# Attention and gated MLP on one core: a new order of the work, the bias loaded first, w_out later, and the last output tiles in two goes

## The chip, the cores and the metric

The kernel runs on one core of a Trainium2 chip. The core has five engines with queues of their own, each of which works its instructions off in order: TensorE (PE in the profile; its weight loads are PEld) for matmuls, VectorE (DVE), ScalarE (ACT), GpSimd (POOL) and SyncE (SP), which here only issues DMAs. The metric is the device time of one execution in microseconds (us), the median of several runs.

## The reference, cut to what matters

Four batches, eight heads, 768 positions, head size 64; the positions form eight blocks of 96.

```python
P = sort_net                                    # [4, 8, 8, 8]
for _ in range(5):                              # Sinkhorn
    P = np.exp(P - P.max(-1, keepdims=True))
    P = P / P.sum(-1, keepdims=True)
    P = P / P.sum(-2, keepdims=True)
k_sorted = einsum('bhij,bhjcd->bhicd', P, k_b)  # blocks of k and v mixed by P
v_sorted = einsum('bhij,bhjcd->bhicd', P, v_b)
scores = q_b @ k_sb.T / 8                       # inside each block of 96
x = softmax(scores) @ v_sb                      # then heads side by side: [4, 768, 512]

h = relu(x @ w_in)                              # [4, 768, 1024]
u, v = h[..., :512], h[..., 512:]
v_n = (v - mean(v)) / sqrt(var(v) + 1e-6)
v_s = einsum('ts,bsd->btd', w_spatial, v_n) + b_spatial[None, :, None]
out = (u * v_s) @ w_out                         # [4, 768, 512]
```

## The kernel before, in words

The work is cut into small units, functions named `u_XX`, and the string `ORDER` lists them one after another: `SC:2:1:0:1` calls `u_SC` with the PSUM bank 2, batch 1, head pair 0, half 1. The order is written out by hand; no scheduler moves anything. Each engine gets its instructions in the order in which the units issue them, and waits only where data or a buffer are not ready. So a unit that stands early in the list and whose data are late holds back everything behind it on its engine. A letter A, D or P in a unit names the engine that takes the result out of PSUM or works on it: ScalarE, VectorE or POOL. PSUM has eight banks, used mostly in pairs (0, 2, 4, 6).

The units of one batch:

- Loads (`L`, `LH`, lines 152 to 212) are issued by POOL and cast from fp32 to bf16 on the way. `LH` loads q by four heads.
- Head of the program only: `SK` is one Sinkhorn step (one exp on ScalarE, six operations on VectorE), `MK` makes a mask, `SX` a selector, `PR` (line 258) spreads P with eight small matmuls, `P0` (line 265) multiplies the mask by P into `pd[0]`, the mixing matrices of batch 0, on VectorE. `PC` copies the spread P to SBUF and `PD` makes the matrices of batches 1 to 3 on POOL. `DM` are dummy matmuls on a zero tile.
- `QT` (318) turns q of a head pair, `KT` (346) mixes and turns k, each with 12 matmuls and one copy. `VT` (357) does the same with v of batch 0 and `VX` (374) turns it back by halves into `vb`. For batches 1 to 3, `VM` (386) mixes v of a head pair in two matmuls and `VC` (400) moves it to `vb` by four DMAs of 99 KB on SP's queue, one for each block; `VC:b:0` and `VC:b:1` are the halves.
- For batches 2 and 3, `QX` (171) replaces `QT`: q is reordered by two copies (VectorE or POOL) and turned by one DMA transpose on SP's queue. `WT` (302) is a one-element copy on POOL that waits for that transpose, so that the loads behind it on POOL do not start before.
- `SC` (410) makes the scores of a head pair and half of the blocks (8 matmuls) and their exp on ScalarE, `AT` (439) multiplies them with `vb` (8 matmuls, line 448, one for each block and head) and divides by the sums (VectorE, or ScalarE, VectorE and POOL for P).
- x is turned by `XT` (TensorE, batch 0) or `XX` (DMA transpose on SP's queue, the others).
- `VP` (484) computes the v half of x @ w_in, one or two tiles of 128 positions, relu, statistics; `LN` the root, `LA` (515) normalizes a tile in place; `UP` (528) computes the u half; `WS` (293) turns w_spatial.
- `SP` (543) computes one quarter of w_spatial @ v_n in 12 matmuls, adds the bias (`z`, line 554) and multiplies by u (`gt`, 560): the gate. `SH` (563) does this for one half of the positions. `OP` (591) computes two tiles of the output from the four gates of a batch, copies and stores them; `OH` (579) one tile.

The batches overlap: attention of batch b+1 is interleaved with the MLP of batch b. SP's queue holds, in order, the load of P, the eight `VC` of batch 1, the bias, then for each batch two `XX`, the q transpose, the eight `VC`, and the output stores. The last units are `SP:6:D:3:2 SP:4:D:3:0 SP:6:P:3:1 SH:4:D:3:3:1 SH:5:D:3:3:0`, then six `OH`.

Of the kernel before, what the change touches and what calls it, by code (L numbers as in the profile page):

```python
# [8 lines left out]
FP32 = mybir.dt.float32  # L9
# [51 lines left out]
def kernel(  # L61
# [34 lines left out]
    moe = ctx.enter_context(tc.tile_pool(name="moe", bufs=2))  # L96
# [33 lines left out]
    mask16 = const.tile([128, TB], BF16, name="mask16")  # L130
# [100 lines left out]
    def u_MK():  # L231
        nc.vector.reduce_sum(out=m32, in_=ident.rearrange("p (j t) -> p t j", t=TB), axis=AX.X)
        nc.vector.tensor_copy(out=mask16, in_=m32)
        for n in range(NE):
            nc.vector.memset(ex[n][:, 2 * NI * BLK:], 0.0)

    def u_IV(n):
        n = int(n)
# [35 lines left out]

    def u_PC(eng):
# [287 lines left out]
    def u_SH(ps, gate, b, mc, x):  # L563
# [12 lines left out]
        eng = nc.vector if gate == "D" else nc.gpsimd  # L576
        eng.tensor_mul(out=st["gt", b, mc][:, cols], in0=z, in1=st["u", b, mc // 2][:, mc % 2, cols])

    def u_OH(ps, eng, b, c):
        b, c = int(b), int(c)  # L580
        t = ps_tile(ps)
        for mc in range(FC):
            nc.tensor.matmul(
                t[:, 0, :], lhsT=st["gt", b, mc][:, c * 128:(c + 1) * 128], rhs=w_out_sb[:, mc, :],
                start=(mc == 0), stop=(mc == FC - 1),
            )
# [58 lines left out]
```

## Time and profile before

| | us |
|---|---|
| median of 13 runs | 159.59 (158.27 to 162.24) |
| profiled execution | 159.21 |
| its span | 157.2 |
| TensorE busy | 141.8 |
| VectorE, ScalarE, POOL busy | 118.0, 83.5, 53.8 |
| first matmul, last matmul's end | 6.5, 152.7 |

The span runs from the first instruction to the last; the rest of the 159.21 us lies around it. Matmuls overlap in time, so a busy TensorE is not TensorE at its peak; chains of units are better read from the timeline. A DMA's row (`SPq`, or POOL for the loads) is the time in which it is issued; its landing comes later and is shown by whoever waits for it.

### The profile page before, as it was taken

The numbers are of one execution on the slowest core, as the hardware profiler recorded it, in microseconds if no ns is written. First come the engines' busy times: TensorE is split into PE (matmuls) and PEld (weight loads), VectorE is DVE, ScalarE is ACT, GpSimd is POOL, SyncE is SP. The second block draws the span as 40 slices with busy tenths as digits, with TensorE's granted clock in tenths as the row PEclk, the third lists the DMA queues.
The fourth block names the chain that finished last, engine by engine and source line by source line (L and its number), as shares of the span: only waits on it lengthen the run. The fifth ranks groups of instructions, "written<-read, shape, count | busy, mean of one in ns | idle before, by whom it ended". The sixth has DMA issues, their size and how long they took to land.

```text
span 157.2 us, 3919 instructions
## 1 busy us (share of the span) xinstructions
PE 141.8 (90%) x1617; PEld 88.3 (56%) x1617; DVE 118.0 (75%) x231; ACT 83.5 (53%) x127; POOL 53.8 (34%) x78
## 2 busy tenths in 40 slices
PE   0399989899998999999899979999999999999880
PEld 0397878546776665645556644655566545556330
DVE  3865889599896789489786999775688679649830
ACT  3234989588877526666654325787751234410130
POOL 7961930747400260240740660062201401500400
PEclk9999999999999999999999999999999999999998
DMA  1999999999999999989999989741554503052073
GB/s 14 194 204 204 207 210 209 203 204 206 243 271 213 205 164 140 201 115 210 216 295 253 154 146 184 123 88 55 216 157 77 100 4 133 0 188 79 0 262 141
DMA packets 36689, 25.49 MB, mean 162 GB/s; under 512 B 16576, under 2 KB 33472, under 8 KB 36672
## 3 DMA queue, kind: packets, MB, share of 16 engines
q0 software_dynamic: 14864, 12.19, 49.9%
q1 hardware_dynamic: 21808, 13.06, 36.1%
q8 instruction: 12, 0.20, 0.5%
q14 instruction: 5, 0.04, 0.1%
HBM read 24.78 MB, written 6.29 MB: 198 GB/s over the span
## 4 chain that ended last, share of the span: by engine, by line
PE 52%; DMA 24%; DVE 11%; POOL 4%; issue 4%; SPq 3%; ACT 1%; DVEq 0%; ACTq 0%; POOLq 0%
PE ps L548 14%; DMA wsp_nat<-in_moe_w_spatial_dram 13%; PE ps L491 10%; PE ps L536 10%; DMA vb<-vm 9%; PE ps L597 8%; DVE z L554 4%; PE ps L448 3%; SPq L405 3%; DVE gt L560 2%; PE ps L423 2%; PE ps L339 2%; DMA out_dram<-oh_sb 1%; DVE stats L505 1%; DVE v_sb L116 1%
## 5 line engine op out<-in xcount | busy, mean ns | idle before, releaser
L548 PE MATMUL ps<-wspT,v_sb 128*128 128x384 bf16 x180 | 31.2, 326 | 0.0
L436 ACT ACTIVATE ex<-ps 96x768 bf16<-96x768 f32 x32 | 24.5, 806 | 10.8 <-PE ps L423 10.8
L536 PE MATMUL ps<-xT,w_in_sb 128*128 128x384 bf16 x128 | 23.0, 326 | 0.8 <-DMA xT<-x_sb 0.5
L491 PE MATMUL ps<-w_in_sb,xT 128*128 128x512 bf16 x96 | 22.7, 379 | 0.5 <-DVE z L554 0.5
L548 PEld LDWEIGHTS <-v_sb 128*128 128x128 bf16 x180 | 17.0, 98 | 10.9
L460 POOL TENSOR_TENSOR x_sb<-xr,rec 96x512 bf16<-96x512 f32 x8 | 8.3, 1040 | 37.7 <-DVE rec L459 37.7
L554 DVE TENSOR_TENSOR z<-ps,b_bc 128x768 f32<-128x768 f32 x15 | 14.3, 953 | 5.4 <-PE ps L548 5.3
L505 DVE BATCH_NORM_STATS2 stats<-v_sb 128x6 f32<-128x512 bf16 x24 | 16.3, 678 | 2.6 <-ACT v_sb L114 2.1
L536 PEld LDWEIGHTS <-w_in_sb 128*128 128x128 bf16 x128 | 12.1, 98 | 9.0 <-issue 1.1
L460 DVE TENSOR_TENSOR x_sb<-ps,rec 96x512 bf16<-96x512 f32 x24 | 16.5, 687 | 0.8
L597 PE MATMUL ps<-w_out_sb,gt 128*128 128x512 bf16 x72 | 16.9, 379 | 0.0
L522 POOL TENSOR_SCALAR v_sb<-v_sb,nm,rstd 128x512 bf16<-128x512 bf16 x15 | 12.1, 806 | 8.5 <-issue 5.4
L491 PEld LDWEIGHTS <-xT 128*128 128x128 bf16 x96 | 9.0, 98 | 10.4 <-issue 0.7
L114 ACT ACTIVATE u_sb<-ps 128x768 bf16<-128x768 f32 x12 | 9.7, 811 | 9.3 <-PE ps L536 9.1
L560 DVE TENSOR_TENSOR gt<-z,u_sb 128x768 bf16<-128x768 f32 x12 | 13.6, 1137 | 0.4
L116 DVE TENSOR_SCALAR v_sb<-ps 128x1024 bf16<-128x1024 f32 (+1 forms) x9 | 9.9, 1100 | 4.5 <-PE ps L491 4.4
L108 ACT CAST vm<-ps 128x768 bf16<-128x768 f32 x11 | 8.5, 804 | 7.6 <-PE ps L390 7.5
L448 PE MATMUL ps<-vb,ex 96*128 96x65 bf16 x256 | 11.9, 193 | 0.7 <-DMA vb<-vm 0.7
L448 PEld LDWEIGHTS <-ex 96*128 96x128 bf16 x256 | 10.0, 97 | 3.5 <-issue 0.9
L521 POOL TENSOR_SCALAR nm<-mv 128x1 f32<-128x1 f32 x15 | 3.0, 199 | 24.7 <-DVE mv L506 18.5
L108 ACT CAST kT<-ps 128x768 bf16<-128x768 f32 x10 | 8.0, 804 | 5.5 <-PE ps L339 5.5
L108 ACT COPY o_sb<-ps 128x1024 f32<-128x1024 f32 x7 | 7.1, 1012 | 6.8 <-PE ps L597 6.6
(91 smaller groups left out, 205.8 us busy)
## 6 DMA issues: line engine op xcount, KB each, us to landing
out_dram<-o_sb SPq DMA_DIRECT2D x9, 512.0 KB, 3.0
k_in<-in_k_dram POOLq DMA_DIRECT2D x4, 768.0 KB, 19.9
v_in<-in_v_dram POOLq DMA_DIRECT2D x4, 768.0 KB, 15.4
vb<-vm SPq DMA_DIRECT2D x24, 99.0 KB, 4.7
q_in<-in_q_dram POOLq DMA_DIRECT2D x3, 768.0 KB, 20.1
out_dram<-oh_sb SPq DMA_DIRECT2D x6, 256.0 KB, 2.0
wsp_nat<-in_moe_w_spatial_dram POOLq DMA_DIRECT2D x1, 1152.0 KB, 20.4
w_in_sb<-in_moe_w_in_dram POOLq DMA_DIRECT2D x2, 512.0 KB, 14.4
```

What stands on the lines that cost most here:

```text
L108: nc.scalar.copy(out=out, in_=in_)
L436: nc.scalar.activation(out=dst, in_=src, func=AF.Exp, scale=scale)
L448: nc.tensor.matmul(t[:, hh, ii * VW:ii * VW + D + 1], lhsT=e[:, c:c + 128], rhs=vb[b % 2][:, ih * NI + ii, 2 * hp + hh, 0:D + 1], start=Tr ...
L460: (nc.gpsimd if eng == "P" else nc.vector).tensor_mul(out=x_sb[:, hp].rearrange("p i (h d) -> p h i d", h=2), in0=tv[:, :, :, 0:D], in1=_r ...
L491: nc.tensor.matmul(t[:, x, :], lhsT=x_tile(b, n // 3)[:, kc, n % 3 * 128:(n % 3 + 1) * 128], rhs=w_in_sb[:, kc, DH:DFF], start=(kc == 0), ...
L505: nc.vector.bn_stats(out=stats, in_=v_sb[:, x, :])
L522: nc.gpsimd.tensor_scalar(out=v_sb, in0=v_sb, scalar1=nm[:, 0:1], scalar2=rs[:, n:n + 1], op0=ALU.add, op1=ALU.mult)
L536: nc.tensor.matmul(t[:, x, 0:HW], lhsT=w_in_sb[:, kc, mc * 128:(mc + 1) * 128], rhs=x_tile(b, ih)[:, kc], start=(kc == 0), stop=(kc == KC ...
L548: nc.tensor.matmul(t[:, x, 0:HW], lhsT=st["v_sb", b, n][:, mc * 128:(mc + 1) * 128], rhs=wspT[:, n, x * HW:(x + 1) * HW], start=(n == 0), ...
L554: nc.vector.tensor_add(out=z.rearrange("p (x c) -> p x c", x=2), in0=t[:, :, 0:HW], in1=b_bc.rearrange("p (x c) -> p x c", x=2),)
L560: eng.tensor_mul(out=gt, in0=z, in1=st["u", b, mc // 2][:, mc % 2])
L597: nc.tensor.matmul(t[:, x, :], lhsT=st["gt", b, mc][:, c * 128:(c + 1) * 128], rhs=w_out_sb[:, mc, :], start=(mc == 0), stop=(mc == FC - 1),)
```

## The change

The string `ORDER` is new from end to end: the same units of attention and MLP in another sequence, with other banks and other engines for some. The parts that have names:

- The bias (`BB`) is issued on SP behind the load of P; it was issued behind the `VC` of batch 1.
- `w_out` (`L:wo`) is loaded behind q of the third batch (b=2) instead of between q of b=1 and v of b=2.
- `P0` takes two heads and all eight rows of P instead of four heads and four rows.
- `VT` mixes a whole head pair's v at once (`ih` = 2: N=128), four units instead of eight with N=64; `VX` stays by halves.
- In the tail, one half of the last gate (`SH:7:D:3:3:1`) stands ahead of the three `SP`, all three of these multiply on VectorE, and the output tiles are made in two goes: `OF` multiplies gates 0 and 1, `OL` adds gates 2 and 3, copies and stores. The last tile is copied by halves, on ScalarE and VectorE, and stored by two DMAs, from ScalarE's queue and SP's.
- q of the fourth batch is reordered by VectorE (`QX:D:3`) instead of POOL; `LA` on POOL goes from 15 to 11, `AT` with P from 8 to 10, `SP` with P from 3 to 5.
- The clearing of the tails of `ex` moves from `u_MK` to `u_IN`.

```diff
-IN SK:0 LH:q:0:0:4 L:k:0:0:128 ID MK SK:0 L:v:0:0:128 SK:0 QT:0:A:0:1:2 SK:0 QT:2:A:0:0:2 DM:0:12:64
-LH:q:0:4:8 DM:1:12:64 SX L:wv DM:0:12:64 DM:1:12:64 SK:1 DM:0:12:64 DM:1:12:64 PR:0 P0:1:4:8 IV:1
-P0:0:4:8 P0:1:0:4 P0:0:0:4 DM:7:5:384 KT:1:A:0:2:2 PC:A KT:3:A:0:3:2 VT:7:D:1:0 IV:0 VT:5:A:2:0
...
-SC:2:0:3:1 PD:1:4:8 SC:0:0:2:1 L:q:1:0:128 L:wo AT:6:D:0:3:0 VX:4:D:2:1 XT:2:A:0:1:0 XT:3:D:0:0:0
-XT:7:D:0:0:1 AT:0:P:0:3:1 L:v:2:0:128 AT:4:D:0:2:1 WS:2:A:1 WS:3:A:3 VP:6:D:0:0:1 XT:0:A:0:1:1
...
-SC:4:1:3:1 LA:P:0:4 BB AT:0:D:1:1:1 UP:2:A:0:1:0 AT:6:D:1:2:1 AT:4:P:1:3:1 SP:0:D:0:1 SC:4:1:2:0
-AT:6:P:1:3:0 SP:2:P:0:0 XX:1:1 AT:6:D:1:2:0 XX:1:0 QX:D:2 VM:4:A:2:0 SP:0:D:0:3 KT:6:A:2:1:2
-VM:4:A:2:3 SP:2:D:0:2 VM:4:A:2:1 VM:0:A:2:2 VP:6:A:1:4:5 UP:0:A:1:1:1 UP:4:A:1:0:0 KT:0:A:2:2:2
-LN:1:4:6 VC:2:0 KT:6:D:2:3:2 KT:2:D:2:0:2 VP:4:D:1:2:3 SC:2:2:2:0 SC:6:2:0:0 VC:2:1 VP:0:D:1:0:1
-WT:q:2:0 L:v:3:0:128 SC:6:2:3:1 SC:2:2:1:0 L:k:3:0:128 OP:4:A:0:2 AT:2:D:2:2:0 L:q:3:0:128 LN:1:0:4
-LA:P:1:1 AT:0:D:2:0:0 LA:P:1:0 LA:D:1:5 OP:6:A:0:1 LA:P:1:4 AT:4:P:2:3:1 UP:2:D:1:0:1 SC:6:2:3:0
...
-SP:6:D:3:2 SP:4:D:3:0 SP:6:P:3:1 SH:4:D:3:3:1 SH:5:D:3:3:0 OH:7:A:3:3 OH:5:D:3:4 OH:4:A:3:0
-OH:7:D:3:5 OH:5:A:3:1 OH:4:A:3:2
+IN LH:q:0:0:4 L:k:0:0:128 ID SK:0 MK L:v:0:0:128 SK:0 SK:0 IV:1 QT:0:A:0:1:2 DM:0:12:64 SK:0
+DM:1:12:64 DM:0:12:64 SK:1 SX DM:1:12:64 QT:2:A:0:0:2 DM:0:12:64 PR:1 P0:0:2 DM:7:9:64 KT:2:A:0:0:2
+LH:q:0:4:8 L:wv P0:2:4 P0:4:6 L:wu IV:0 DM:7:1:64 KT:4:A:0:2:2 P0:6:8 KT:6:D:0:1:2 DM:0:1:64
+VT:2:A:3:2 PC:A L:ws L:v:1:0:128 VT:4:D:0:2 KT:6:D:0:3:2 VX:0:D:3:0 VT:1:A:1:2 QT:4:A:0:3:2 PD:3:0:4
...
+VX:0:D:2:0 XT:1:D:0:1:0 SC:4:0:0:0 XT:2:D:0:1:1 AT:6:D:0:2:0 AT:0:D:0:3:0 AT:4:D:0:0:0 UP:2:A:0:1:1
+VP:7:A:0:5 XT:0:A:0:0:1 WS:2:A:3 XT:4:A:0:0:0 VP:6:D:0:3:4 VM:2:A:1:0 VM:0:A:1:3 VP:4:D:0:2
...
+QT:2:A:1:2:2 LA:P:0:4 QT:6:D:1:1:2 UP:4:D:0:0:0 SC:6:1:3:1 SC:2:1:1:1 WS:0:D:1 L:k:2:0:128 WS:1:D:2
+L:q:2:0:128 SC:4:1:2:1 VC:1:1 QT:6:D:1:0:2 KT:2:A:1:0:2 AT:0:D:1:3:1 LA:P:0:1 SC:4:1:3:0 VC:1:0
+AT:6:D:1:1:1 SC:2:1:0:1 WS:0:D:4 VM:4:A:2:1 AT:6:D:1:2:1 SC:2:1:0:0 LA:P:0:0 L:wo AT:0:D:1:0:1
+LA:P:0:2 SC:4:1:2:0 AT:6:D:1:3:0 LA:P:0:5 AT:2:P:1:0:0 SC:0:1:1:0 KT:4:A:2:1:2 XX:1:1 AT:2:D:1:2:0
+SP:6:P:0:0 AT:4:D:1:1:0 VM:2:A:2:3 XX:1:0 QX:D:2 SP:0:P:0:2 VM:4:A:2:0 VM:2:A:2:2 SP:6:D:0:3
+SP:2:D:0:1 UP:6:A:1:0:1 KT:2:D:2:2:2 KT:0:D:2:3:2 KT:4:A:2:0:2 VP:6:A:1:0:1 UP:0:A:1:1:1 SC:6:2:3:0
+SC:4:2:0:1 VP:2:D:1:4:5 SC:6:2:2:1 VC:2:0 VC:2:1 SC:0:2:3:1 OP:4:A:0:2 AT:0:D:2:3:0 AT:2:D:2:0:1
+LN:1:4:6 VP:6:D:1:2:3 WT:q:2:0 L:v:3:0:128 SC:0:2:1:1 SC:4:2:2:0 L:k:3:0:128 L:q:3:0:128 UP:2:A:1:0:0
...
+UP:2:D:3:0:0 LA:D:3:3 OP:0:A:2:2 LA:P:3:2 SH:7:D:3:3:1 SP:2:D:3:0 SP:0:D:3:1 SP:2:D:3:2 SH:0:D:3:3:0
+OF:7:3:0 OF:2:3:5 OF:3:3:4 OL:A:3:4 OL:D:3:5 OF:0:3:3 OL:A:3:0 OL:D:3:3 OF:2:3:2 OL:A:3:2 OF:7:3:1
+OL:X:3:1
...
     def u_IN():
         nc.sync.dma_start(out=p_all, in_=sort_net.rearrange("b h i j -> (b h) i j"))
...
+        for n in range(NE):
+            nc.vector.memset(ex[n][:, 2 * NI * BLK:], 0.0)
...
-    def u_P0(ih, lo, hi):
+    def u_P0(lo, hi):
...
         nc.vector.tensor_mul(
-            out=pd[0][:, lo:hi, ih * 64:ih * 64 + 64].rearrange("p h (i t) -> p h i t", t=TB),
-            in0=_raw_ap(mask16, 0, [mask16.ap[0], [0, n], [0, NI], [1, TB]]),
-            in1=_raw_ap(pr, lo, [pr.ap[0], [1, n], [BH, NI], [0, TB]]),
+            out=pd[0][:, lo:hi].rearrange("p h (i t) -> p h i t", t=TB),
+            in0=_raw_ap(mask16, 0, [mask16.ap[0], [0, n], [0, NB], [1, TB]]),
+            in1=_raw_ap(pr, lo, [pr.ap[0], [1, n], [BH, NB], [0, TB]]),
         )
...
+    EARLY, LATE = (0, 1), (2, 3)
+
+    def oh_mm(b, c, parts):
+        for mc in parts:
+            nc.tensor.matmul(
+                st["oh", c][:, 0, :], lhsT=st["gt", b, mc][:, c * 128:(c + 1) * 128], rhs=w_out_sb[:, mc, :],
+                start=(mc == EARLY[0]), stop=(mc == LATE[-1]),
+            )
+
+    def u_OF(ps, b, c):
+        st["oh", int(c)] = ps_tile(ps)
+        oh_mm(int(b), int(c), EARLY)
...
+    def u_OL(eng, b, c):
+        b, c = int(b), int(c)
+        oh_mm(b, c, LATE)
+        t = st["oh", c][:, 0]
+        o_sb = oh_tile()
+        dst = out[b, c * 128:(c + 1) * 128, :]
+        if eng in ("A", "D"):
+            copy(eng, o_sb, t)
+            nc.sync.dma_start(out=dst, in_=o_sb)
+        else:
+            h = DM // 2
+            o2 = moe.tile([128, S], FP32, name="o2", tag="z", bufs=2)[:, 0:h]
+            nc.scalar.copy(out=o_sb[:, 0:h], in_=t[:, 0:h])
+            nc.vector.tensor_copy(out=o2, in_=t[:, h:DM])
+            nc.scalar.dma_start(out=dst[:, 0:h], in_=o_sb[:, 0:h])
+            nc.sync.dma_start(out=dst[:, h:DM], in_=o2)
```

## The prediction

> **What bounds the kernel now.** I read the page first, then TensorE's busy time by stage, then its waits, then the queues around the one DMA wait that the change moves, last the end of the timeline.
>
> The page's busy times of the engines:
> ```profile
> PE 141.8 (90%) x1617; PEld 88.3 (56%) x1617; DVE 118.0 (75%) x231; ACT 83.5 (53%) x127; POOL 53.8 (34%) x78
> ```
> Busy time by stage (start:end, length, then the engines in the page's order, granted clock, DMA share, GB/s):
> ```profile
> 6.50:13.40 6.90, 6.65 (x111) 5.88 (x113) 4.72 (x22) 1.88 (x4) 3.96 (x9) 1.00 1.31 204
> 13.40:28.30 14.90, 13.44 (x353) 11.71 (x352) 12.41 (x29) 13.12 (x21) 5.91 (x6) 1.00 1.23 207
> 28.30:138.60 110.30, 108.22 (x1085) 63.93 (x1086) 86.99 (x150) 64.10 (x94) 36.93 (x51) 1.00 0.88 162
> 138.60:157.20 18.60, 13.44 (x73) 6.75 (x71) 10.41 (x12) 2.35 (x4) 1.64 (x1) 0.96 0.38 141
> ```
> From 28.3 to 138.6 us TensorE is busy for 108.2 of 110.3 us: what it loses there is lost for good, and work removed elsewhere is worth nothing. Before 28.3 ScalarE and VectorE are nearly full (13.1 and 12.4 of 14.9) beside full DMAs. The tail is a chain of its own. TensorE's own waits:
> ```profile
> PE ps L324 <- DMA q_in<-in_q_dram: 6.5, 1, 6.5
> PE ps L448 <- DMA vb<-vm: 0.7, 2, 0.4
> PE ps L583 <- POOL gt L560: 0.6, 1, 0.6
> PE ps L536 <- DMA xT<-x_sb: 0.5, 1, 0.5
> PE ps L491 <- DVE z L554: 0.5, 1, 0.5
> ```
> The second line is the one to watch. The third batch's V goes to `vb` by eight DMAs on SP's queue, behind the transpose of q. The timeline of SP and POOL, then TensorE's and the chain's rows:
> ```profile
> 59.25 4.71 SPq L183 DMA_TRANSPOSE qX<-qx  x1
> 64.05 5.99 SPq L405 DMA_DIRECT2D vb<-vm  x8
> 65.51 0.18 POOL L305 COPY gate<-qX 1x1 bf16<-1x1 bf16 x1 [7.21 <-DMA qX<-qx]
> 66.03 0.95 POOL L156 DMA_DIRECT2D v_in<-in_v_dram  x1 [0.34 <-PE ps L536]
> ...
> 68.86 7.33 DMA vb<-vm
> ...
> 76.23 0.31 PE L448 MATMUL ps<-vb,ex 96*128 96x65 bf16 x5 [0.40 <-DMA vb<-vm]
> ```
> The last block is issued at 68.86 and lands at 76.19, 16.9 us after the q transpose began to issue. The load of the last batch's v is let go by that same transpose (through the gate copy) and its packets run beside the second half of `vb`. TensorE reached that block just in time and lost 0.4 us.
>
> **The change, part by part.** The sum is made against the profiled execution (span 157.2, 159.21 us, 0.4 under the median 159.59).
>
> *Bias first.* b_bc (384 KB) issues on SP at 1.15, where p_all's issue ends (0.74+0.41). Output DMAs land in 3.0 us for 512 KB and 2.0 for 256 KB, so 384 KB cost at most 1.5 us of transfer; at least 0, if all is over before q's data flows. POOL has issued q by 2.21, 1.06 later; so I take 1.5-1.06=0.4. ScalarE's fourth Sinkhorn exp stands behind the first qT copy, which waits for q: q used at 6.47, exp at 8.06 where VectorE was done at 7.77. The 0.4 goes into the head's chain whole. Removed at 41 us: nothing waited for it there.
>
> *P by head pairs.* Four products of 128x256 (0.416 us each) before and after; the first KT follows one of them instead of two: at 12.56+0.4+0.42=13.4, as before (13.37).
>
> *First V whole.* 96 matmuls of N=64 (2.6 us) become 48 of N=128 (7.1/192 each, 1.8). Copies, by rows: VectorE 3 vT of 0.549 and 1 kT of 0.946 become 2 vT (priced as kT of that shape) and 2 kT; 7 vb become 6: 15.3 to 16.1 us from P0 to the last AT. ScalarE: 5 vT of 0.494, 3 kT of 0.804, 1 vb become 2, 2 and 2: 14.5 to 13.4. Together 29.8 against 29.5, no gain. Walking the copies in order with the 0.4, TensorE begins its unbroken stream (UP of the second half of batch 0) at 28.1, against 28.33; between 27.5 (no idle time on VectorE after P0) and 29.2 (bias at its dear end). Dummies: 71 of 64 columns for 72, and the five of 384 columns (1.0) go; they lie under the Sinkhorn chain, so 0.
>
> *w_out later.* It leaves the slot between q1 and v2. 512 KB at 204 GB/s is 2.6 us: v2, k2, q2 come that much earlier, w_out last, used from 68. Nothing waited for v2 to q2 before. In the new order the third batch's first VM stands at 48.7: v loads land 10.5 to 22.8 us after issue, so v2 (issued 29.47 before) at 52.3 at the latest, 2.6 earlier now, 1.0 late; by the median of 15.4, in time. I take 0 (bounds 0 and 1.0). k2, q2 and w_out issue behind LA steps on POOL (38 to 43); the loads ahead of them keep the DMAs full until then.
>
> *The new order, stream.* TensorE's units, by the chain and timeline: SP 1.97, OP 1.76, UP 1.32, VP 0.87 a tile, WS 0.43, XT 0.42, KT and QT 0.40, VM 0.34, SC 0.25, AT 0.24. Summed in the order before from 28.33 to the first SP of the tail (106.98): 135.31; real 138.56, so 3.25 of waits: 1.4 up to the first OP (second batch's attention), 0.6 at `vb`, 1.3 at 88 to 96 (xT, and a gt of 3.10 us beside POOL's qx). After: one XT more, 107.40, from 28.1.
> Waits after, by walking all engines through the rows: the second batch's attention now has eight exps, two KT, VM and xr packed on ScalarE (9.4 us) over 6.3 us of TensorE: 2.2 up to the first OP (1.4 before; 0.8 to 3).
> Then `vb`. The last AT of batch 1 (AT:4:D:1:1:0) is on TensorE at 54.9+0.4, VectorE done 57.0; qx (1.9, now next on VectorE) 58.9; transpose issue at 59.0; last block lands 59.0+16.9=75.9. TensorE gets from that AT to AT:2:D:2:0:1 (which needs the last block) after one VP pair less than before: 17.3 us of units from 55.3 and 0.1 of waits: 72.7. **Wait: 3.2, with 0.1 behind it 3.3.** Bounds: landing takes 2.7 to 7.6 us after issue over the 24 `vb` rows; at 2.7 after an issue at 68.6 the block is there at 71.3 and the wait is 0; at 7.6, 3.5. I take the 7.33 of this very transfer, as v3 is let go by the same event and runs beside it again. Behind the wait stand a VP pair, UP, OP, all in order; ScalarE and VectorE only idle.
> The 1.3 at 88 to 96 goes: QX:3 leaves POOL for VectorE (0.97 a copy), and XX:2:1 is issued before the VP that needs it. In its place 0 (up to 1.3). LA (15 to 11 on POOL), two gt and two AT more on POOL: cover remains, POOL has 103 us idle.
> Tail begins at 28.1+107.4+2.2+3.3=141.0, against 138.56: **+2.4**.
>
> *Tail.* The rows:
> ```profile
> 145.65 1.64 POOL L560 TENSOR_TENSOR gt<-z,u_sb 128x768 bf16<-128x768 f32 x1 [8.14 <-DVE z L554]
> 147.35 5.36 PE L583 MATMUL ps<-w_out_sb,gt 128*128 128x512 bf16 x23 [0.61 <-POOL gt L560]
> ```
> From its first matmul the tail took 14.15 us on TensorE (138.56 to 152.71) for 13.1 of units: it waited for POOL's gt (1.64) and two SH gates. After, SH goes first, all gates on VectorE (0.96 each), and six matmuls on parts 0 and 1 run while gates 2 and 3 finish: VectorE ends gate 2 at +9.0 and gate 3 at +10.2, TensorE needs them at +9.2 and +10.1. So 13.1: -1.0. The last copy is half a tile on two engines: 0.59 becomes 0.43 (0.692 less half of 1.225-0.692), -0.2. Its DMA: halves with the bandwidth to themselves would land in 1.5 instead of 2.0 (-0.5); if they share, 0. I take 0, since all 256 KB still move. [...] Tail: **-1.2**.
>
> Sum: +2.4-1.2=+1.2 us: 158.4 span, 160.4 in that execution, **160.8** against the median.
>
> A long wait has a second price. The row of 152.7 to 157.2 us, without a matmul, has a mean granted clock of 0.83, so, if it falls to half, it fell for about 1.5 of 4.5 us, some 3 us after the last matmul. The wait above is 3.2 us, broken by three blocks that land before, so I take 0; at most +1.6, if the clock then stayed at half as long as the wait. [...]
>
> **The rivals.**
> *The wait does not come (other side).* If the second half of `vb` lands before 72.7, the sum is +1.2-3.3=-2.1: 157.5. For: the third batch's `vb`, without a load beside it, is among the 2.7 to 4.7 us rows. Against: v3 begins by the same trigger. It decides where the last block takes under 4.1 us from issue, or VectorE finishes qx 3 us earlier.
> *Half a wait.* ScalarE's packed stretch or the head delays TensorE while q's transpose is early: wait 1.5 to 2: 159.5, no change within the 0.5% (0.8 us) that a measurement of this kernel tells apart. For: both hang on the same AT, so only VectorE's order between them matters; against: that order is fixed.
> *Dearer.* Bias at 1.5 us, or a slow clock after the wait: +1.1 or +1.6 more: 161.9 to 162.4. Against: the bias has a head start.
> *The change does nothing* is excluded: TensorE's order is new throughout.
>
> **How the numbers follow.** Likeliest 0.52 (159.7 to 162.0 on its own), no wait 0.26, half 0.12, dearer 0.10. Range 157.0 to 162.6: it leaves out the upper half of the dearer case and the cheap end of no wait. Slower: 0.45 of the likeliest and all of the dearer, 0.55; same: 0.07 and 0.11, 0.18; faster 0.27.
>
> **What would show it.** L448 waiting for DMA vb<-vm by about 3 us near 73 to 76; qX issued within 1 us of 59; the q load landing near 6.9; no wait at 88 to 96; from the tail's first SH to the last L584 matmul 13.1 us. I am wrong if TensorE's wait at vb is under 1.5 us, if the head starts its stream after 29.2, or if a new wait over 1 us stands elsewhere.

## The result, and the profile after

The changed kernel takes 162.69 us (median of 11 runs, 160.46 to 164.76) against 159.81 us for the kernel before (48 runs): ratio 1.0144, 95% interval 1.0104 to 1.0183. It is slower, as predicted, by 2.3 us by the ratio and 2.9 by the medians instead of 1.2, and the median lies 0.1 us above the top of the predicted range. Executions of one kernel differ in the mean granted clock of TensorE, and the ratios, here and below, leave out the slow executions, so that they differ from those of the medians. Of the twelve executions of the changed kernel six have a mean granted clock of 0.989 to 1.00 and spans of 158.7 to 160.9 us; the other six, with the profiled one among them (span 163.2, clock 0.974, time 164.99), have 0.973 to 0.980 and 161.4 to 163.2 us.

Against the predicted span of 158.4 the profiled execution has 4.8 us more. About 2.5 of them are the price of the half clock, as shown below, and belong to such executions alone. Stage by stage:

| stage (us) | predicted | after, profile | difference |
|---|---|---|---|
| TensorE's stream begins (first UP) | 28.1 | 29.82 | +1.7 |
| from there to AT:2:D:2:0:1 | 44.6 | 43.55 | -1.05 |
| that AT's waits for `vb` | 3.3 | 3.76 | +0.45 |
| from its end to the first SH | 64.8 | 67.3 | +2.5 |
| first SH to last matmul | 13.1 | 13.14 | 0 |
| last matmul to end | 4.3 | 5.4 | +1.1 |

The head, in the timelines of SP, TensorE and ScalarE (start, duration in us, engine, line, operation, and in brackets the idle time before it and who ended it):

```profile
1.20 0.41 SPq L222 DMA_DIRECT2D b_bc<-in_moe_b_spatial_dram  x1
...
8.90 0.85 PE L324 MATMUL ps<-ident,q_in 128*64 128x128 bf16 x12 [8.90 <-DMA q_in<-in_q_dram]
...
10.49 0.25 ACT L244 ACTIVATE p_all<-p_all 32x64 f32<-32x64 f32 x1
...
29.82 1.46 PE L536 MATMUL ps<-xT,w_in_sb 128*128 128x384 bf16 x8
```

q lands at 8.90 where it landed at 6.47; the fourth Sinkhorn exp follows at 10.49 (8.06 before). The stream starts 1.7 us later than forecast.

SP's, POOL's and TensorE's timelines around the third batch's `vb`:

```profile
59.68 4.02 SPq L183 DMA_TRANSPOSE qX<-qx  x1
63.80 6.85 SPq L405 DMA_DIRECT2D vb<-vm  x8
...
66.25 0.95 POOL L156 DMA_DIRECT2D v_in<-in_v_dram  x1 [0.34 <-issue]
...
73.13 0.41 PE L448 MATMUL ps<-vb,ex 96*128 96x65 bf16 x8
74.26 0.20 PE L448 MATMUL ps<-vb,ex 96*128 96x65 bf16 x1 [0.72 <-DMA vb<-vm]
75.61 0.19 PE L448 MATMUL ps<-vb,ex 96*128 96x65 bf16 x1 [1.14 <-DMA vb<-vm]
76.31 0.22 PE L448 MATMUL ps<-vb,ex 96*128 96x65 bf16 x1 [0.51 <-DMA vb<-vm]
77.13 0.44 PE L448 MATMUL ps<-vb,ex 96*128 96x65 bf16 x5 [0.60 <-DMA vb<-vm]
77.37 3.60 PE L491 MATMUL ps<-w_in_sb,xT 128*128 128x512 bf16 x8
```

AT:2:D:2:0:1 begins behind the AT of 73.13, at 73.37, and takes its four blocks as they land; the next unit starts at 77.37, which is 4.00 us for a unit of 0.24: 3.76 of wait. Then the eight matmuls of L491 take 3.60 us instead of 1.89. TensorE's own waits and the windows (length, busy time and count of PE, PEld, DVE, ACT, POOL, then the granted clock, DMA share and GB/s) say why:

```profile
PE ps L324 <- DMA q_in<-in_q_dram: 8.9, 1, 8.9
PE ps L448 <- DMA vb<-vm: 3.0, 4, 1.1
```

```profile
72.00:77.00 5.00, 2.15 (x17) 1.08 (x16) 2.65 (x7) 2.30 (x5) 0.00 (x0) 0.91 1.24 225
77.00:79.00 2.00, 1.87 (x9) 0.84 (x9) 0.89 (x2) 0.00 (x0) 0.00 (x0) 0.50 1.24 250
79.00:81.00 2.00, 2.00 (x7) 0.55 (x7) 0.00 (x0) 0.00 (x0) 0.00 (x0) 0.50 1.19 271
81.00:83.00 2.00, 2.00 (x21) 1.27 (x22) 1.92 (x2) 1.49 (x2) 0.00 (x0) 0.53 1.32 205
83.00:86.00 3.00, 3.00 (x36) 1.79 (x35) 1.67 (x6) 1.71 (x6) 0.56 (x1) 1.00 0.54 83
```

The granted clock is 0.50 until nearly 83. The trace gives the fall at 76.05 and the return at 82.88, so the clock fell inside the wait, 1.3 us before its end. VP, two SC and UP take 6.2 us behind it (77.37 to 83.58); at a clock of 1.00, in e2 below, the same units take 3.6 (72.94 to 76.57). The waits that the kernel before had at 88 to 96 us are gone, as forecast. At the end, the timeline of ScalarE, VectorE and SP:

```profile
157.85 0.37 ACT L613 COPY o_sb<-ps 128x256 f32<-128x256 f32 x1 [0.23 <-PE ps L584]
158.25 2.23 ACTq L615 DMA_DIRECT2D out_dram<-o_sb  x1
158.25 0.42 DVE L614 COPY o<-ps 128x256 f32<-128x256 f32 x1 [1.44 <-ACT o_sb L613]
158.70 0.34 SPq L616 DMA_DIRECT2D out_dram<-o  x1
```

The two half copies run one after the other, not beside each other, and the store issued by ScalarE takes 2.23 us to issue; SP issues the other half in 0.34.

### The profile page after: what moved, and what is told of

Same layout as the page of the kernel before. It is cut to its first block, busy times and chain, and to the rows that moved or that the text cites. A ratio compares the mean times of both kernels' runs of the same rounds, so it can differ in the third digit from the quotient of the medians.

```text
span 163.2 us, 3811 instructions
## 1 busy us (share of the span) xinstructions
PE 143.5 (88%) x1563; PEld 89.1 (55%) x1563; DVE 114.2 (70%) x230; ACT 85.8 (53%) x129; POOL 53.0 (32%) x72
## 4 chain that ended last, share of the span: by engine, by line
PE 77%; DMA 9%; DVE 5%; SPq 3%; ACT 2%; issue 2%; DVEq 0%; POOLq 0%
PE ps L548 18%; PE ps L536 13%; PE ps L491 12%; PE ps L628 9%; DMA q_in<-in_q_dram 5%; PE ps L448 4%; DMA vb<-vm 4%; PE ps L423 4%; PE ps L339 3%; PE ps L584 3%; SPq L405 3%; PE ps L390 2%; PE ps L324 2%; PE ps L290 2%; PE ps L378 1%
## 5 line engine op out<-in xcount | busy, mean ns | idle before, releaser
L460 POOL TENSOR_TENSOR x_sb<-xr,rec 96x512 bf16<-96x512 f32 x10 | 10.6, 1065 | 43.8 <-DVE rec L459 27.3
L491 PE MATMUL ps<-w_in_sb,xT 128*128 128x512 bf16 x96 | 24.4, 400 | 0.1
L536 PE MATMUL ps<-xT,w_in_sb 128*128 128x384 bf16 x128 | 24.0, 332 | 0.0
L108 ACT COPY o_sb<-ps 128x1024 f32<-128x1024 f32 (+1 forms) x10 | 9.3, 927 | 13.6 <-PE ps L584 9.3
L460 DVE TENSOR_TENSOR x_sb<-ps,rec 96x512 bf16<-96x512 f32 x22 | 15.1, 686 | 0.8
L491 PEld LDWEIGHTS <-xT 128*128 128x128 bf16 x96 | 9.4, 102 | 10.5 <-issue 1.6
L324 PE MATMUL ps<-ident,q_in 128*64 128x128 bf16 x96 | 4.6, 244 | 8.9 <-DMA q_in<-in_q_dram 8.9
L522 POOL TENSOR_SCALAR v_sb<-v_sb,nm,rstd 128x512 bf16<-128x512 bf16 x11 | 9.0, 822 | 9.1 <-issue 4.1
L114 ACT ACTIVATE v_sb<-ps 128x1024 bf16<-128x1024 f32 (+1 forms) x7 | 6.7, 963 | 7.7 <-PE ps L491 7.6
L423 PEld LDWEIGHTS <-kT 64*96 64x96 bf16 x256 | 8.1, 124 | 4.8 <-issue 3.4
L116 DVE TENSOR_SCALAR v_sb<-ps 128x1024 bf16<-128x1024 f32 (+1 forms) x6 | 6.8, 1130 | 5.4 <-PE ps L491 5.4
```

Of the source, the lines that this page charges most:

```text
L114: nc.scalar.activation(out=out, in_=in_, func=AF.Relu)
L423: nc.tensor.matmul(t[0:BLK, hh, ii * 128:ii * 128 + BLK], lhsT=kT[rows, i * BLK:(i + 1) * BLK], rhs=rhs, start=True, stop=True,)
L460: (nc.gpsimd if eng == "P" else nc.vector).tensor_mul(out=x_sb[:, hp].rearrange("p i (h d) -> p h i d", h=2), in0=tv[:, :, :, 0:D], in1=_r ...
L491: nc.tensor.matmul(t[:, x, :], lhsT=x_tile(b, n // 3)[:, kc, n % 3 * 128:(n % 3 + 1) * 128], rhs=w_in_sb[:, kc, DH:DFF], start=(kc == 0), ...
L536: nc.tensor.matmul(t[:, x, 0:HW], lhsT=w_in_sb[:, kc, mc * 128:(mc + 1) * 128], rhs=x_tile(b, ih)[:, kc], start=(kc == 0), stop=(kc == KC ...
```

## The experiments

Theory: the main loss is that TensorE's new order comes too early to data whose landing is fixed by the DMAs. To it come three parts whose prices were set too low: the bias first, the clock after the wait, and the split last tile. Rivals: the landing follows TensorE, so that the order isn't at fault; the clock falls for another reason; the parts cost nothing by themselves. All kernels compute the whole output. Times are set against the kernel before on the same chip.

**The changed kernel again, and three parts undone, on one chip** (before 159.48 us). First the same kernel, which is the measure for the others:

> The changed kernel itself, its order only wrapped into other lines. In its first profile TensorE waited 3.7 us for the last vb block of the third batch and then ran at a granted clock of 0.50 until 82.9 us, about 2.7 us lost; the mean clock of its other executions lies between 0.97 and 1.00. Expected here: 160 to 164 us, a wait of 3 to 4 us before 77 us, the stream starting at 29.8 us, and a spread that follows the mean clock by about 1.6 us for 0.01.

163.32 us, ratio 1.0233 (1.0171 to 1.0295); the profile, at a clock of 0.973, has a span of 161.8. q lands at 7.96 and the stream begins at 28.56; qX issues at 59.46; TensorE leaves the waiting AT at 76.11, and the next eight L491 matmuls take 3.60 us again; last matmul to end 5.3 us. The wait (3.75 us: 3.99 from start to start, less the unit's 0.24) and the half clock repeat (a mean of 0.65 in 74 to 76 us, 0.50 from 76 to 80, 0.64 in 80 to 82, so from about 74.6 to 81.4); the bias's price is smaller here.

e2: v3 let go by the landing of all of `vb` instead of that of qX:

```diff
+    def u_WV(b):
+        nc.gpsimd.tensor_copy(out=gate[0:1, 0:1], in_=vb[int(b) % 2][0:1, NB - 1, 0, 0:1])
-WT:q:2:0 L:v:3:0:128
+WT:q:2:0 WV:2 L:v:3:0:128
```

> Changed kernel, but the load of the fourth batch's v (and k and q behind it) waits on POOL until the last vb block of the third batch has landed. Theory 1 (v3's packets crowd the second half of vb): the last block lands 2.7 to 4.7 us after its issue near 70, that is at 72 to 74.5 instead of 77.2, TensorE's wait falls from 3.7 to under 1 us, the clock stays at 1.0, and the time falls by 3 to 6 us to 156 to 158, unless v3, about 5 us later, is now late for the VM of the fourth batch near 90. Rival (the vb transfers are slow by themselves, or the wait has another cause): the wait stays at 3 us or more and the time at 160 or above.

162.0 us, ratio 1.0085 (1.0027 to 1.0143): less gained than the 156 to 158 us that were expected. In the profile (span 157.9, clock 0.991) the wait of the `vb` matmuls is gone (they stand at L451 here), the load of v3, let go by the last block, issues at 71.6, 8.3 us after the first block's issue at 63.27, and the clock is 1.00 from 28 to 139. In the changed kernel the last block landed 13.3 us after the first issue (77.1 and 63.80). So the loads beside the transfer are what made it late. But the loads are now late themselves, and run beside the transposes of the third batch's x, for which TensorE then waits:

```profile
72.46 0.65 PE L451 MATMUL ps<-vb,ex 96*128 96x65 bf16 x16
...
94.07 1.90 PE L494 MATMUL ps<-w_in_sb,xT 128*128 128x512 bf16 x8 [1.76 <-DMA xT<-x_sb]
```

Its other runs have spans of 158.4 to 160.8 at clocks of 0.98 to 1.0, so the profiled one is the fastest; what differs in them isn't known.

e3: bias back behind `VC:1:0`:

```diff
-AT:4:D:0:2:1 BB AT:2:P:0:1:0
+AT:4:D:0:2:1 AT:2:P:0:1:0
-VC:1:0 AT:6:D:1:1:1
+VC:1:0 BB AT:6:D:1:1:1
```

(In the changed list `BB` stands behind `AT:4:D:0:2:1`, but nothing of SP's lies between P's load and it, so it issues at 1.20.)

> Changed kernel with the bias issued behind the vb transfers of batch 1 again. Theory 1 (the bias ahead of q delayed q from 6.5 to 8.9 us and with it the fourth Sinkhorn step and the whole head): q lands near 6.5, the stream starts near 28.0 instead of 29.8, the vb wait stays at 3 to 4 us, and the time falls by 1.5 to 2 us. Rival (the price of 0.4 us that the prediction put on it; the rest of the late head is the new order): the stream starts at 29.4 and the time falls by 0.4 us.

162.81 us, ratio 1.0161 (1.0063 to 1.026). q lands at 6.42 and the stream begins at 27.13: 1.4 us better than the run beside it. In the time next to nothing of that arrives (162.81 for 163.32 us, ratios within each other's intervals; the profile's span is 162.7 for 161.8). SP's timeline:

```profile
50.18 9.10 SPq L190 DMA_TRANSPOSE xT<-x_sb  x2
59.38 3.61 SPq L183 DMA_TRANSPOSE qX<-qx  x1
63.09 1.27 SPq L405 DMA_DIRECT2D vb<-vm  x2
```

The transposes start 1.4 us earlier and the q transpose issues where it issued before: 59.38 for 59.46. The waits for `vb` take the gain (2.9 us in the view of waits there, 5.8 here). What holds the transposes seems to be the loads: in eight profiles of the new order (the changed kernel twice, e1 to e3, e10 to e12) w_out, the last of the loads to be issued, landed between 58.2 and 59.5 us, whether it was issued at 41.9 or at 44.5, and in these eight, e4 and e5 qX issued between 59.1 and 60.3. No run moved the end of the loads, so that they are the cause is inferred.

e4: last tile whole, by ScalarE and one DMA of SP:

```diff
-OL:X:3:1
+OL:A:3:1
```

> Changed kernel, but the last output tile is copied by ScalarE in one piece and stored by SP. Theory 1 (the half stored from ScalarE's queue takes 3.6 us to land, where the tiles before took 2.0 to 2.4): from the last matmul to the end of the span 4.4 us instead of 5.4, the time 0.9 us lower. Rival (the split is worth its copy of half the length, as the prediction had it): 0.2 us higher.

162.74 us, ratio 1.0206 (1.0122 to 1.029), against 1.0233 for the same kernel with the split tile: within the intervals. The profiles say it more sharply: last matmul to end 4.7 us for 5.3.

```profile
156.20 1.20 SPq L609 DMA_DIRECT2D out_dram<-o_sb  x2
...
156.41 0.59 ACT L108 COPY o_sb<-ps 128x512 f32<-128x512 f32 x1 [0.23 <-PE ps L584]
```

**The order alone, and the clock alone** (one execution each, before 159.39 us). e1: the AT behind the VP that follows it:

```diff
-AT:2:D:2:0:1 LN:1:4:6 VP:6:D:1:2:3
+LN:1:4:6 VP:6:D:1:2:3 AT:2:D:2:0:1
```

> The changed kernel with the AT that needs the last vb block (AT:2:D:2:0:1) put behind the VP that follows it, so that eight matmuls of L491 (1.89 us at full clock, 1.74 from first to next) run before it. Nothing that sets the transfers moves. Theory (the wait is TensorE's order against a fixed landing): in the changed kernel run again TensorE came to this AT at 72.97 and its last block at 75.86, 2.9 us of waits; now it comes at 74.7, the wait is 1.1 to 1.4, too short for the clock to fall, and the profile's rows of L491 beside it keep 1.89 us. Against the span of 161.8: -1.7 of wait and -1.9 to -2.7 of clock, 157.2 to 158.2. Rival A (the gain is given back at the next transfer, xT of the third batch, because the loads of the last batch pin it as they pin the transposes of the second): a new wait of 1 to 2 us for xT near 94 to 98, span 159 to 160. Rival B (the landing follows TensorE, since both hang on the same instruction): the wait stays 2.5 to 3, span 161 to 162.

160.65 us, span 158.9 at a clock of 0.998. TensorE's timeline:

```profile
72.23 1.89 PE L491 MATMUL ps<-w_in_sb,xT 128*128 128x512 bf16 x8
73.96 0.46 PE L448 MATMUL ps<-vb,ex 96*128 96x65 bf16 x2
75.35 0.19 PE L448 MATMUL ps<-vb,ex 96*128 96x65 bf16 x1 [0.93 <-DMA vb<-vm]
76.08 0.31 PE L448 MATMUL ps<-vb,ex 96*128 96x65 bf16 x5 [0.54 <-DMA vb<-vm]
76.32 0.56 PE L423 MATMUL ps<-qX,kT 64*96 64x96 bf16 x16
77.99 1.46 PE L536 MATMUL ps<-xT,w_in_sb 128*128 128x384 bf16 x8 [1.11 <-DVE x_sb L460]
```

The AT is left at 76.32, as before the edit (76.11), with a VP done meanwhile: the landing does not follow TensorE (rival B falls), and the clock stays at 1.00 through 73 to 100. There is no new wait for xT (rival A falls). But 1.1 us of the gain went to a wait that no theory had: the AT's division now stands behind the VP's relu and statistics on VectorE (2.9 us), and UP needs the AT's bank.

e5: dummies in the wait:

```diff
-AT:0:D:2:3:0 AT:2:D:2:0:1
+AT:0:D:2:3:0 DM:2:14:384 AT:2:D:2:0:1
```

> The changed kernel with 14 matmuls of 384 columns put before the AT that waits for vb (into a bank that nothing reads); the output is the same. They take about 14 x 0.165 = 2.3 us, 72.97 to 75.3, inside the wait that ended at 75.86 in the changed kernel run again. They separate the wait from its clock. Theory (idle time halves the granted clock): the last block lands as before, near 75.9, the wait is cut to 0.6 us and less, the granted clock stays at 1.0 in 74 to 82 (it was 0.50 to 0.65 for 6 to 7 us), the VP behind it takes 1.89 us and not 3.60; span 161.8 - 2.3 (to -2.7) = 159.1 to 159.5. Rival (the clock falls for another reason than this idle time, such as power under the DMAs): 0.5 again near 76 to 82, span 161.5 to 162.

161.31 us, span 159.5 at a clock of 0.999. Timeline, then the windows:

```profile
72.82 2.44 PE L290 MATMUL ps<-warm 128*128 128x384 bf16 x14
...
76.16 0.31 PE L448 MATMUL ps<-vb,ex 96*128 96x65 bf16 x5 [0.51 <-DMA vb<-vm]
76.31 1.89 PE L491 MATMUL ps<-w_in_sb,xT 128*128 128x512 bf16 x8
```

```profile
77.00:79.00 2.00, 2.00 (x25) 1.04 (x24) 1.20 (x2) 0.45 (x1) 0.00 (x0) 1.00 1.20 273
79.00:81.00 2.00, 1.95 (x18) 1.17 (x18) 1.91 (x4) 1.92 (x4) 0.00 (x0) 1.00 1.24 247
```

The last block is met at nearly the same time (76.16 for 75.86), the wait is as long, and the clock doesn't fall: L491 takes 1.89 us. The span is 2.3 us shorter than that of the unfilled kernel's profile although nothing useful was moved. That the idle time brings the half clock down on this stretch fits all profiles of the new order: the clock fell inside the wait in the four with 2.9 us or more of waits for `vb` (the changed kernel twice, e3, e4), and in none of the six with 1.5 us or less. But e1 and e5 are one execution each; e10 below idles 3.1 us at almost the same place, in another wait, without a fall; and six of the changed kernel's twelve executions have a mean clock of 0.989 or more, too high for a fall of this length (6.83 us at half is 0.021 of the mean over 163.2 us). So the price is often paid, not always, and the idle time alone doesn't explain it.

**The tail alone** (e9): the kernel before with the changed `OF`/`OL` tail, last tile whole.

```diff
-SP:6:D:3:2 SP:4:D:3:0 SP:6:P:3:1 SH:4:D:3:3:1 SH:5:D:3:3:0 OH:7:A:3:3 ... OH:4:A:3:2
+SH:7:D:3:3:1 SP:2:D:3:0 SP:0:D:3:1 SP:2:D:3:2 SH:0:D:3:3:0 OF:7:3:0 ... OF:7:3:1 OL:A:3:1
```

> The kernel before, with the changed kernel's tail alone (SH first, all gates on VectorE, the last tiles in two goes), but the last tile written whole by one DMA. Theory (the tail's order is worth its 1.0 us of TensorE, and the split last tile only cost): from the first matmul of the tail to the last 13.1 us for 14.15, from the last matmul to the end 4.5 to 4.6 as before: -1.0 us, ratio 0.993 to 0.995. Rival A (the new tail gains only behind the changed kernel's order, where other engines are freer): 13.8 to 14.2 us, ratio 0.998 to 1.002. Rival B (the split tile is worth something, so that its loss shows): the end 0.3 to 0.5 longer than before, ratio 0.996 to 0.998.

158.81 us against 159.39, ratio 0.9947 (0.9906 to 0.9988). First matmul of the tail to the last 13.15 us (141.31 to 154.46) for 14.15, then 4.7 to the end. The tail's order is a gain by itself, of about what was worked out for it.

**The bias (e7) and w_out (e8) alone, in the kernel before** (one execution each):

```diff
-LA:P:0:4 BB AT:0:D:1:1:1
+LA:P:0:4 AT:0:D:1:1:1
-IN SK:0
+IN BB SK:0
```

> The kernel before with the bias load as first load on SP's queue and nothing else moved. Theory (its broadcast rows hold q back): q lands at 7.9 to 8.9 for 6.47, the fourth exp and the stream start come 1.4 to 2.4 later (29.7 to 30.7 for 28.33), span +0.5 to +1.5 as the waits of the second batch's attention and of vb take up the rest. What the prediction took: 0.4 at each.

Span 159.4 at a clock of 0.997, against 157.2 at 0.995: +2.2. Timelines of TensorE and ScalarE:

```profile
8.69 1.49 PE L324 MATMUL ps<-ident,q_in 128*64 128x128 bf16 x24 [8.69 <-DMA q_in<-in_q_dram]
...
10.27 0.25 ACT L244 ACTIVATE p_all<-p_all 32x64 f32<-32x64 f32 x1
...
30.18 0.83 PE L297 MATMUL ps<-ident,wsp_nat 128*128 128x128 bf16 x12
```

q is 2.2 us late, the exp 2.2, the stream 1.85. Here all of it reaches the end, more than expected; but it is one execution, and the kernel before at clocks of 0.988 and over has spans of 156.5 to 158.8 on this chip, so 0.6 to 2.9 us is what can be said.

```diff
-L:q:1:0:128 L:wo AT:6:D:0:3:0
+L:q:1:0:128 AT:6:D:0:3:0
-L:q:2:0:128 KT:6:A:1:2:2
+L:q:2:0:128 L:wo KT:6:A:1:2:2
```

> The kernel before with w_out's load issued behind that of the third batch and nothing else moved: v2, k2 and q2 come 2.6 us earlier, w_out last. Theory (nothing waited for any of them, and the DMAs are full to the same end): no TensorE wait comes or goes by over 0.3 us, span 157 to 157.5 at a full clock. Rival (the earlier k2, q2 let the transposes start earlier): qX issued before 58, last vb block before 75, span up to 0.5 less.

Span 159.0, but at a clock of 0.972: it stood at half from about 23.7 to 30.5 us (0.92 in 22 to 24, 0.50 from 24 to 30, 0.87 in 30 to 32), at the end of the head, where the one profile of the kernel before shows 1.00.

```profile
22.00:24.00 2.00, 1.10 (x25) 0.98 (x25) 0.95 (x4) 1.04 (x3) 0.00 (x0) 0.92 1.16 211
24.00:26.00 2.00, 2.00 (x36) 1.67 (x34) 1.59 (x5) 1.21 (x2) 0.00 (x0) 0.50 1.15 210
26.00:28.00 2.00, 2.00 (x32) 1.91 (x29) 1.53 (x4) 1.56 (x3) 0.00 (x0) 0.50 1.28 203
```

The kernel before with only the new tail shows the same stretch (0.58, 0.50, 0.50 from 24 to 30), so it isn't w_out's doing. From the stream's start to the tail it is 110.7 us for 110.2 in the kernel before, with 0.7 more of a wait for xT: in this one execution nothing is gained and at most 0.5 lost. qX issues 31.1 us after the stream's start for 30.9 before: no earlier transposes.

**Putting it right.** e10: the four edits together, with v3 let go by the fifth block rather than the last:

```diff
+        nc.gpsimd.tensor_copy(out=gate[0:1, 0:1], in_=vb[int(b) % 2][0:1, 4, 0, 0:1])
-AT:2:D:2:0:1 LN:1:4:6 VP:6:D:1:2:3 WT:q:2:0 L:v:3:0:128
+LN:1:4:6 VP:6:D:1:2:3 AT:2:D:2:0:1 WT:q:2:0 WV:2 L:v:3:0:128
```

(and `BB` behind `VC:1:0`, `OL:A:3:1`)

> The changed kernel with four edits: the bias load back at its place before (behind VC:1:0), the AT that needs the last vb block behind the VP that follows it, the load of v3 let go by the landing of the fifth vb block (a one-element copy on POOL) and not by that of qX, and the last tile written whole. Theory (what the change loses is these four, and each of them is independent): the head's stream starts at 27.1 for 28.6, v3 issues near 68 to 69, 3 us later than in the changed kernel and 3 earlier than where it waited for the whole of vb; the last block lands at 71 to 73, TensorE comes at 73.3, wait 0 to 0.3, clock 1.0 throughout, no wait over 0.5 us for xT at 88 to 96; last matmul to end 4.6: span 154.5 to 155.5, ratio 0.985 to 0.990. Rival A (the DMAs are the bound from 28 to 95, so that what TensorE gains early it waits for at the next transfer): stream at 27.1, but 1.5 to 3 us of waits for vb or for xT, span 156.5 to 158, ratio 0.997 to 1.005. Rival B (v3 later makes k3 and q3 late too): waits of TensorE for k_in or v_in after 95, span over 158.

160.17 us, ratio 1.0039 (1.0003 to 1.0075); span of the profile 157.0, of the other nine 156.9 to 159.8. In the profile there is no wait for `vb`, none for xT, none for k or v, so neither rival came. One wait stands in TensorE's timeline:

```profile
73.09 0.56 PE L426 MATMUL ps<-qX,kT 64*96 64x96 bf16 x16
76.78 1.46 PE L539 MATMUL ps<-xT,w_in_sb 128*128 128x384 bf16 x8 [3.14 <-DVE x_sb L463]
```

It is VectorE's queue behind the moved AT again (e1), 3.1 us now that the landing no longer covers it. So the edit that shortened the wait by itself is the wrong one here. e11, without it:

```diff
-WT:q:2:0 L:v:3:0:128
+WT:q:2:0 WV:2 L:v:3:0:128
```

> The kernel of four edits without one of them: AT:2:D:2:0:1 stands ahead of the VP again, as in the changed kernel; bias back, v3 let go by the fifth vb block, last tile whole. In the kernel of four edits the eight vb blocks landed from 66.0 to 71.4, TensorE did not wait for them at all, and the AT behind the VP had its copies behind the VP's relu and statistics on VectorE, for which TensorE waited 3.14 us. Theory (that queue on VectorE is the whole of the new wait): TensorE comes to the AT at 71.0, waits 0.4 for the last block, then nothing until 92: span 157.0 - 3.1 + 0.4 = 154.3, up to 155, ratio 0.980 to 0.986. Rival (the loads, now 3 us later than before, pin the next transfer): 1 to 1.8 us of wait for xT near 91 to 94, as where v3 waited for the whole of vb (1.8), span 155.5 to 156.5, ratio 0.988 to 0.995.

156.28 us (155.68 to 157.51, 4 runs) against 160.19 for the kernel before on that chip: ratio 0.9826 (0.9743 to 0.991). This version beats both. POOL's and TensorE's timelines of the profile, whose span of 155.7 is the longest of the four (the others 153.9 to 154.7):

```profile
69.30 0.18 POOL L309 COPY gate<-vb 1x1 bf16<-1x1 bf16 x1 [4.16 <-DMA vb<-vm]
69.85 0.96 POOL L156 DMA_DIRECT2D v_in<-in_v_dram  x1 [0.36 <-issue]
...
70.72 0.65 PE L451 MATMUL ps<-vb,ex 96*128 96x65 bf16 x16
71.21 1.89 PE L494 MATMUL ps<-w_in_sb,xT 128*128 128x512 bf16 x8
...
92.60 1.90 PE L494 MATMUL ps<-w_in_sb,xT 128*128 128x512 bf16 x7 [2.03 <-DMA xT<-x_sb]
```

Both AT follow one another without a wait for `vb`, and the VP behind runs at full clock; but in the profiled run the rival's wait for xT is there, 2.0 us. The theory gave 154.3 and the rival 155.5 to 156.5: the profile goes with the rival, the other three spans with the theory. Last, e12, the same with the bias first again:

```diff
-VC:1:0 BB AT:6:D:1:1:1
+VC:1:0 AT:6:D:1:1:1
-AT:4:D:0:2:1 AT:2:P:0:1:0
+AT:4:D:0:2:1 BB AT:2:P:0:1:0
```

> As e11_v3_half_at_front, with the bias as first load again: the price of this part where no wait for vb hides it. The changed kernel run again had its q at 7.96 and its stream at 28.56, with the bias back 6.42 and 27.13. Theory (a later head is lost for good unless a transfer that is pinned elsewhere absorbs it): stream 1.4 later, of which the wait of 0.4 for the last vb block is saved: +1.0 us against e11_v3_half_at_front. Rival (the DMAs pin everything behind 59 us): 0 to +0.3.

157.62 us (156.85 to 158.22), ratio 0.9891 (0.9801 to 0.9981). By the medians the bias costs 1.3 us, by the profiles 0.4 (156.1 against 155.7): the stream begins 1.9 later (29.07 for 27.21), and the wait for xT falls from 2.0 to 0.7. Both theories work at once, and four runs of each don't settle the shares.

## Why the prediction was right or wrong

*The direction and its cause: right.* The wait for `vb` was foreseen at its place and at 3.3 us and measures 3.76 and 3.75 in two profiles; with the load moved it is gone, and with the order moved it shrinks. The wait is that of the likeliest case; the median of 162.69 us is not within that case's 159.7 to 162.0. Both conditions of the dearer rival, which was given a chance of 0.10, were met as well in the profiled executions: a bias at about 1.5 us or more, and a slow clock after the wait. The stream's start at 29.82 is also past the 29.2 that the prediction named as a sign of being wrong (28.56 in the second profile is not), and q landed at 8.90 and 7.96 for 6.9. That the time still came within 0.1 us of the range is in part luck, since errors cancelled.

*What sets the landing: right number, half wrong reason.* The prediction put the q transpose at 59.0 because VectorE's qx copies end at 58.9. It issued at 59.7 and 59.5. With the bias back the copies end at 57.2 and it issues at 59.38 all the same, behind transposes that the loads seem to hold until 59. So a faster head lengthens the wait: 5.8 us in the view of waits there for 2.9.

*Bias first: the term of 0.4 was mis-sized.* It holds q back by 1.5 to 2.5 us in the changed order (7.96 and 8.90 for 6.42) and by 2.2 in the kernel before, and the stream by 1.4 to 2.7 (28.56 and 29.82 for 27.13). The step at fault is that a head start of 1.06 us covers all but 0.4 of the transfer; its length was taken from rows of output stores, 1.5 us for 384 KB, while this load took 5.0 us from issue to landing. The profile before had a row for this very load, issued at 41.0 and landed 8.0 us later, and it was not used. Without the bias the new head starts its stream at 27.1 to 27.3, about half a microsecond before the 27.7 that the prediction's walk gives without its 0.4; no run took that apart.

*Slow clock: the term of 0 was mis-sized.* By the stage behind the wait, 64.8 us in the forecast, it was worth 2.5 us in this profile (67.3) and 2.4 in the next (67.2); without that the profile's span would be near 160.7 us, and the one execution with a mean clock of 1.00 has 160.3. The prediction reasoned that single blocks break the wait. They did not protect the clock; in the one execution with the wait filled by matmuls it stayed at 1.00. The clock fell when the longest gap behind it was 1.14 us (1.83 in the second profile). It also cost more than the 1.6 that was allowed: the clock stood at half for 6.83 us, 5.5 of them behind the wait.

*Split last tile: the terms 0 and -0.2 were mis-sized.* Two queues were taken to share the same bandwidth, at no cost, and the two half copies to run side by side. But ScalarE's issue took 2.23 us where SP's took 0.34, and VectorE's half copy, behind 1.44 us of idle time, waited for ScalarE's: +1.1 in all against the forecast, of which the whole tile brings back 0.7 in the profiles. So the second issuing engine cost issue time here, where the forecast has none.

*The second batch's packed attention: the term of 2.2 us was too high by about 1.1* (43.55 us in the profile and 43.56 in the second one, for 44.6). That is luck: it hid a part of the other errors. No run took it apart.

*Right as worked out:* the tail at 13.1 us of units (13.14; 13.15 in the kernel before with that tail), no waits at 88 to 96, and, by one execution, w_out later at nothing.

## What to carry to other kernels

Before a consumer is moved forward, find what sets the landing of its data: here the q transpose ahead of its transfers issued at 59.1 to 60.3 us, near the landing of w_out (58.2 to 59.5), whatever came before, so a head that was 1.4 us earlier brought 0.5 us by the medians (e3), and delaying the next loads by 4 us until half of the transfer had landed brought 1.7% over the kernel before, with the tail's gain and the other repairs. A unit that is moved behind another moves on every engine's queue, and the queue that it then waits in may not be the one that was considered (VectorE's here, 1.1 us in e1 and 3.1 in e10). A load of a few hundred KB that isn't needed soon should not stand ahead of the first data of the critical path (384 KB held q back by 1.5 to 2.5 us here), and a wait of 3 to 4 us of TensorE should be priced with the half clock that can come with it (2.4 to 2.5 us here, in the two profiles of the changed kernel).

## What the runs showed of the hardware that was not expected

- The granted clock did not go by the length of a gap alone. It fell in the changed kernel, at 76.05 us, when TensorE had been waiting for 2.5 us, broken by two single matmuls, with 1.14 us as the longest gap. It fell near 24 us of the kernel before with the new tail (e9) and of that with w_out later (e8), where the longest gap was 0.8 and 0.9 us and TensorE was busy for 1.24 and 1.10 us of the 2 from 22 to 24. It stayed at 1.00 beside an unbroken gap of 3.14 us (e10).
- The falls in the midst of the work were of nearly one length. In the changed kernel the trace has 61.44 us at 1.00, 6.83 at 0.50 and 78.51 at 1.00; in its second profile, e3, e4, e8 and e9 the windows of 2 us give 6.8 us each (e9: 0.58 in 24 to 26, 0.50 from 26 to 30, 0.71 in 30 to 32). The kernel before has 143.36 us at 1.00 without a fall. No run shows what sets the moment or the length.
- A 128 KB store issued by ScalarE, the only one on its queue, took 2.20 to 2.23 us to issue and 3.6 to land (the changed kernel twice, e3); SP's of the same size took 0.33 to 0.34 and 2.1 to 2.2.
- Eight SBUF-to-SBUF transfers of 99 KB, whose first issued at 63.8, were not all there before 77.1 with three loads of 768 KB let go in their midst from 66.3 on. In e11, where the first issued at 62.9 and the loads were let go from 69.9 on, TensorE found all eight landed when it came at 71.0.
